# Block-sparse attention into a split-precision MLP on one core: the absolute value of the weight conversion, the fetches of the second matrix and the copies of P are issued at other places

## The chip, the cores and the metric

One core of a Trainium2 chip runs the whole program. The metric is device time in microseconds of one execution: the lower, the better. TensorE (PE) multiplies, with its weight loads shown as PEld; VectorE (DVE), ScalarE (ACT) and GpSimd (POOL) do the rest, and DMAs are issued from the queues of SyncE (SP), POOL and ACT.

## What is computed

Attention over 4 batches, 8 heads, 768 positions of 64 values, with a block mask (blocks of 32: neighbours, first and last block row and column, and three sampled blocks for each row of blocks), and behind it a two-matrix MLP with a sigmoid gate:

```python
scores = np.where(mask, scale * np.matmul(q, k.transpose(0, 1, 3, 2)), -1000000000.0)
attn = np.exp(scores - np.max(scores, axis=-1, keepdims=True))
attn = attn / (np.sum(attn, axis=-1, keepdims=True) + 1e-09)
attn_out = np.matmul(attn, v)
x = attn_out.transpose(0, 2, 1, 3).reshape(B * S, H * D)      # 3072 x 512
h = x @ w_in                                                  # 512 x 2048
g = h * (1.0 / (1.0 + np.exp(-1.702 * h)))
return g @ w_out                                              # 2048 x 512
```

The two weight matrices reach the kernel as 64-bit floating-point words, and the kernel turns them itself into pairs of 32-bit numbers.

## The kernel before

The 3072 tokens are worked on in six chunks of 512. The MLP of a chunk runs over 16 slices of the 2048 inner features; one slice is one turn of `tick(m)`, so ticks 0 to 15 are the first chunk. A tick has four quarters. `up(m)` multiplies the chunk by slice m of `w_in` (12 matmuls), `gate(m)` forms the product g (a tanh on ACT, a copy of the bank to SBUF on ACT in ticks 0 to 12, a multiplication on DVE), and `down(m - 1)` multiplies the slice before by its slice of `w_out`. From slice 8 on g is split: `gate_hi` is a cast on ACT, `gate_lo` a subtraction on DVE at the start of the next tick, and `down` has 12 matmuls of which the last four (line 635) need the low part of g.

Attention of the next chunk is woven in by `plan`, which gives quarters of ticks to its parts. In the first chunk an item's scores stand in quarters 8, 14, 20, 26, 32, 38, 44, 50 and 56, its transposes four quarters behind, and with the scores of an item go the values of the item before (64 small matmuls, line 379). Scores (line 304) and transposes (line 355) use the same two PSUM banks, 0 and 1: the scores can start only when `pt`, ACT's two copies of the transposed P (line 360), has left both. The smallest score is found on DVE (line 327), the four exponentials follow on ACT (line 339). After the last transposes of an item `turn` copies the normalised output into x: a high part on ACT (line 455), a low part on DVE (line 456).

In the same ticks the weights are converted by a generator, `weights()`, `self.conv` in `tick`. It has 32 steps k, in `todo`: step 0 is slice 0 of `w_in`, odd k are slices (k + 1) / 2 of `w_in`, even k are slices k / 2 - 1 of `w_out`, and step 31 is the last slice of `w_out`. A step asks for words to come (`fetch`, a 512 KB DMA on POOL's queue), shifts the absolute value of step k (line 515, DVE), rounds the word of step k - 1 (`rounded`, line 496, ACT), subtracts for its low part (`rest`, line 500, DVE), puts the sign in (line 521, DVE), takes the absolute value of step k + 1 (`first`, line 493, ACT), and puts the low bits in (line 529, DVE). Slices of `w_out` are also written back to DRAM from SP's queue (`ws`, line 535). Slices 0 to 7 of `w_out` need no rounding. `yield` stands between these parts, and `tick` says how many yields are run at each place: `n0` behind the first quarter, `n1` inside `gate`, between the copy of the bank and the multiplication, `n2` at the end. They are 0, 4, 2 in ticks 5, 8, 11 and 14; 2, 4, 4 in ticks 3, 6, 9 and 12; 2, 4, 3 in ticks 4, 7, 10, 13 and 15; 0, 4, 2 in tick 2.

Before the absolute value of a slice f of `w_out` the generator yields as long as the ring of finished slices has no room; `self.downs` is m in tick m once `down(m - 1)` has been issued, and `down` stands between `gate` and the `n2` yields:

```python
while todo[k + 1][1] == 1 and (not self.turned or todo[k + 1][0] - (4 if todo[k + 1][0] < NFULL else WRING) > self.downs - 1):
    yield
```

The tile `a` of the absolute value has two buffers, so from step 18 on that of step k + 1 takes the place of that of step k - 1. The words of `w_out` come into `raw`, which has three buffers; from slice 8 on the converted word stays in it until it has been written back and split. POOL's queue also holds the gathers of the sampled rows of V (line 256), two for each pair of items, issued in `begin` when the values of an item have let go of their buffers.

In ticks 4, 7, 10 and 13 the transposes and the `turn` stand in the third quarter, and there the two copies of P and the copies of `turn` are issued inside `gate`. Everything is issued in the order of the program on each engine.

Of the kernel before, what the change touches and what calls it, by code (L numbers as in the profile page):

```python
# [13 lines left out]
ALU = mybir.AluOpType  # L14
# [24 lines left out]
BIG = float(2 ** 33)  # L39
SCALE = 1.0 / float(D) ** 0.5  # L40
REBASE = 2.0 ** -112
AHEAD = 5
NFULL = 8
FIRST = CU // 2
ORDER = """G0 G1 G2 G3 S0 L0 E0 S1 L1 T0 E1 X1 C0 S2 T1 C1 L2 S3 V0 V1 L3 E2 N0 X2 N1 R0 Y3 E3 T2 R1 X3 C2 H1 T3 H0 S4 Y1 L4 S5 L5
# [4 lines left out]
class Kernel:  # L50
# [411 lines left out]
    def weights(self):  # L462

        nc = self.nc
        todo = []
        for f in range(NF + LAG):
            if f < NF:
                todo.append((f, 0))
            if f >= LAG:
                todo.append((f - LAG, 1))  # L470
        self.ready = set()
        tiles = {}

        def fetch(k):
            if k < len(todo):
                f, i = todo[k]
                if i == 0:
                    raw = self.const.tile([P, 2 * DM], I32, name=f"win{f}")
                else:
                    raw = self.work.tile([P, 2 * DM], I32, name="raw", bufs=3)  # L480
                nc.gpsimd.dma_start(out=raw, in_=self.w64[i][f])
                tiles[k] = {"raw": raw.rearrange("p (a b) -> p a b", b=2)}

        def first(k):


            f, i = todo[k]
            if i == 0 or f >= NFULL:
                a = self.work.tile([P, DM], I32, name="a")
            else:  # L490
                a = self.work.tile([P, DM], F32R, name=("ghi", "glo")[f % 2]).bitcast(I32)
            tiles[k]["a"] = a
            nc.scalar.activation(out=a.bitcast(F32), in_=tiles[k]["raw"][:, :, 1].bitcast(F32), func=AF.Abs, scale=REBASE)

        def rounded(k):
            nc.scalar.copy(out=tiles[k]["to"][:, 0:DM], in_=tiles[k]["w"])

        def rest(k):
            t, w = tiles[k]["to"], tiles[k]["w"]
            nc.vector.tensor_tensor(out=t[:, DM:2 * DM], in0=w, in1=t[:, 0:DM].bitcast(F32), op=ALU.subtract)  # L500
            self.ready.add(todo[k])

        for k in range(3):
            fetch(k)
        yield
        for k in range(3, AHEAD):
            fetch(k)
        yield
        first(0)
        yield  # L510
        for k, (f, i) in enumerate(todo):
            fetch(k + AHEAD)
            raw, a = tiles[k]["raw"], tiles[k]["a"]
            low, high = raw[:, :, 0], raw[:, :, 1]
            nc.vector.tensor_scalar(out=a, in0=a, scalar1=3, scalar2=None, op0=ALU.logical_shift_left)
            if k > 0 and "to" in tiles[k - 1]:
                rounded(k - 1)
                yield
                rest(k - 1)
            yield  # L520
            nc.vector.scalar_tensor_tensor(out=a, in0=high, scalar=-0x80000000, in1=a, op0=ALU.bitwise_and,
                                           op1=ALU.bitwise_or)
            if k + 1 < len(todo):
                while todo[k + 1][1] == 1 and (not self.turned or todo[k + 1][0] - (4 if todo[k + 1][0] < NFULL else WRING) > self.downs - 1):
                    yield
                first(k + 1)
            yield
            w = a if (i, f >= NFULL) != (1, True) else raw.rearrange("p a b -> p (a b)")[:, 0:DM]
            nc.vector.scalar_tensor_tensor(out=w, in0=low, scalar=29, in1=a, op0=ALU.logical_shift_right,
                                           op1=ALU.bitwise_or)  # L530
            w = tiles[k]["w"] = w.bitcast(F32)
            if i == 0:
                self.win[f] = tiles[k]["to"] = self.const.tile([P, 2 * DM], F32R, name=f"win{f}")
            else:
                nc.sync.dma_start(out=self.ws[f], in_=w)
                if f < NFULL:
                    self.whole[f] = w
                    self.ready.add((f, i))
                else:
                    tiles[k]["to"] = self.wout[f % WRING]  # L540
            yield
        rounded(len(todo) - 1)
        rest(len(todo) - 1)
        yield
# [195 lines left out]
    def tick(self, m):  # L740

        n0, n1, n2 = 0, 0, 0
        if m < NF:
            has = lambda part, at: any(part == p for q in at for p, g in self.at.get(q, ()))
            quarter = QT * m
            heavy = has(self.scores, range(quarter, quarter + QT))
            n0, n1, n2 = (0, 4, 4) if heavy else ((2, 2, 5), (2, 4, 1))[m] if m < 2 else (2, 4, 3)
            if has(self.transposes, [quarter]) and heavy:
                n0 = 2
            if has(self.transposes, [quarter + QT]) and has(self.scores, [quarter]):  # L750
                n2 = 2

        def run(n):
            for _ in range(n):
                next(self.conv, None)

        def finish(todo):
            for f in todo:
                f()

        moe = m < NC * NF
        self.gate_lo(m - 1)
        after = self.begin(QT * m)
        finish(after)
        run(n0)
        if moe:
            self.up(m, range(0, 2))
        finish(self.begin(QT * m + 1))
        if moe:
            self.up(m, range(2, 4))  # L770
        after = self.begin(QT * m + 2)
        parts = [[part for part, g in self.at.get(QT * m + q, ())] for q in (2, 3, 4)]
        if m < NF and self.turn in parts[0] and self.values in parts[1] + parts[2]:
            self.gate(m, lambda: (run(n1), finish(after[:2] + after[3:])))
            after = after[:3]
        elif moe:
            self.gate(m, lambda: run(n1))
            finish(after[:2])
        else:
            finish(after[:2])  # L780
        self.down(m - LAG, 0)
        if moe:
            self.gate_hi(m)
        finish(after[2:])
        finish(self.begin(QT * m + 3))
        self.down(m - LAG, 1)
        self.split(m + 1)
        self.stream(m + 3)
        run(n2)
# [141 lines left out]
```

## Time and profile before

| | |
|---|---|
| median of 3 runs | 755.73 us (755.47 to 756.55) |
| the profiled execution, its own time | 755.67 us |
| its span | 754.0 us |
| PE busy | 730.1 us (97%) |
| DVE busy, ACT busy, POOL busy | 405.6 us (54%), 375.7 us (50%), 70.4 us (9%) |
| DMA | 126.87 MB, mean 168 GB/s |

Times in the trace are counted from the start of the span. A row of a timeline gives the start, the length, the engine, the line of the kernel, the operation with its output and inputs, and in brackets how long the engine was idle before it and what ended that. The instructions of one engine overlap at their ends, so two starts may be closer than the length of the first.

### The profile page before, as it was taken

How to read it: one execution, taken by the hardware profiler on the slowest of the kernel's cores; microseconds unless marked ns; L12 is line 12 of the kernel's file. 1: busy time of each engine (PE TensorE's matmuls, PEld its weight loads, DVE VectorE, ACT ScalarE, POOL GpSimd, SP SyncE). 2: the span in 40 equal slices, each digit the busy share in tenths (PEclk: the TensorE clock that was granted, in tenths of full speed). 3: DMA queues.
4: the chain of work that ended last, by engine and by line, in shares of the span. 5: the costliest groups of instructions: out<-in, count | busy, mean ns of one | idle time of the engine just before them, and what ended most of it. 6: DMA issues, size and time to landing. Idle time of an engine off the chain costs nothing.

```text
span 754.0 us, 18913 instructions
## 1 busy us (share of the span) xinstructions
PE 730.1 (97%) x7424; PEld 562.6 (75%) x7424; DVE 405.6 (54%) x1069; ACT 375.7 (50%) x939; POOL 70.4 (9%) x111
## 2 busy tenths in 40 slices
PE   3989999999999999999999999999999999999997
PEld 1665667777787777788778778778777777888885
DVE  3778879885554445454454454354555344443332
ACT  2766667765464454444445445444554454333232
POOL 4333212120000000000000000000000000000000
PEclk9999999999999999999999999999999999999999
DMA  8999996685642547554444564445564321041111
GB/s 240 304 372 363 334 329 200 228 254 176 237 162 82 170 155 212 154 178 149 122 150 147 150 172 155 127 141 155 185 222 141 106 77 43 30 112 43 56 43 56
DMA packets 64250, 126.87 MB, mean 168 GB/s; under 512 B 7617, under 2 KB 30402, under 8 KB 63650
## 3 DMA queue, kind: packets, MB, share of 16 engines
q1 hardware_dynamic: 51922, 83.72, 36.0%
q0 software_dynamic: 11376, 41.03, 16.1%
q8 instruction: 58, 0.95, 0.5%
q10 hardware_dynamic: 864, 0.93, 0.4%
q14 instruction: 30, 0.25, 0.1%
HBM read 115.16 MB, written 10.49 MB: 167 GB/s over the span
## 4 chain that ended last, share of the span: by engine, by line
PE 92%; DVE 3%; ACT 2%; issue 1%; DMA 1%; SPq 0%; ACTq 0%
PE bank L579 12%; PE bank L580 11%; PE bank L581 11%; PE bank L639 11%; PE bank L635 11%; PE bank L640 11%; PE bank L304 6%; PE bank L355 6%; PE bank L379 5%; PE bank L624 3%; PE bank L399 2%; PE bank L316 2%; PE bank L448 2%; DMA scratch<-in_sampled_blocks_dram 1%; DMA vmid<-in_v_dram 1%
## 5 line engine op out<-in xcount | busy, mean ns | idle before, releaser
L594 DVE SCALAR_TENSOR_TENSOR g<-g,bank 128x512 f32<-128x512 f32 x83 | 57.1, 688 | 169.3 <-ACT g L587 169.2
L339 ACT ACTIVATE ex<-bank,nm 128x256 f32<-128x256 f32 (+1 forms) x176 | 84.8, 491 | 119.8 <-DVE nm L327 119.8
L639 PE MATMUL bank<-wout,ghi 128*128 128x512 f32 x352 | 139.2, 396 | 0.0
L640 PE MATMUL bank<-wout,ghi 128*128 128x512 f32 x352 | 136.7, 388 | 0.0
L587 ACT ACTIVATE g<-bank 128x512 f32<-128x512 f32 x96 | 57.6, 600 | 147.0 <-PE bank L581 147.0
L562 DVE TENSOR_TENSOR wout<-wst,wout 128x512 fp32r<-128x512 f32 x80 | 55.4, 692 | 78.9 <-ACT wout L561 77.9
L635 PE MATMUL bank<-wout,glo 128*128 128x512 f32 x352 | 97.0, 388 | 0.0
L327 DVE CUSTOM_DVE_ANT_1 bank<-bank,bias 128x256 f32<-128x256 f32 x176 | 73.7, 440 | 21.4 <-PE bank L304 9.7
L579 PE MATMUL bank<-xhi,win 128*128 128x512 f32 x192 | 79.7, 415 | 0.5 <-ACT xhi L455 0.5
L601 ACT CAST ghi<-g 128x512 fp32r<-128x512 f32 x88 | 54.8, 623 | 47.7 <-DVE g L594 47.7
L579 PE MATMUL bank<-x,win 128*128 128x512 f32 x192 | 77.7, 405 | 0.0
L635 PEld LDWEIGHTS bank<-wout,glo 128*128 128x128 f32 x352 | 66.1, 188 | 13.9
L639 PEld LDWEIGHTS bank<-wout,ghi 128*128 128x128 f32 x352 | 66.1, 188 | 13.0
L640 PEld LDWEIGHTS bank<-wout,ghi 128*128 128x128 f32 x352 | 66.2, 188 | 12.8
L580 PE MATMUL bank<-xlo,win 128*128 128x512 f32 x192 | 74.9, 390 | 0.0
L581 PE MATMUL bank<-xhi,win 128*128 128x512 f32 x192 | 74.8, 390 | 0.0
L581 PE MATMUL bank<-x,win 128*128 128x512 f32 x192 | 74.7, 389 | 0.0
L580 PE MATMUL bank<-x,win 128*128 128x512 f32 x192 | 74.7, 389 | 0.0
L256 POOL DMA_INDIRECT vown<-in_v_dram,vidx x40 | 39.9, 997 | 371.9 <-PE bank L379 258.5
L360 ACT COPY pt<-bank 128x512 f32<-128x512 f32 (+1 forms) x112 | 57.0, 565 | 20.3 <-PE bank L355 20.2
L304 PE MATMUL bank<-kg,qt 64*32 64x256 f32 x1280 | 48.4, 399 | 13.3 <-DMA vmid<-in_v_dram 11.9
L609 DVE TENSOR_TENSOR glo<-g,ghi 128x512 fp32r<-128x512 f32 x88 | 60.3, 685 | 1.4 <-ACT ghi L601 1.4
(140 smaller groups left out, 1047.8 us busy)
## 6 DMA issues: line engine op xcount, KB each, us to landing
wst<-ws SPq DMA_DIRECT2D x80, 256.0 KB
kg<-in_kb_dram SPq DMA_DIRECT2D x114, 128.0 KB
kg<-in_kb_dram SPq DMA_DIRECT2D x42, 256.0 KB
win<-in_moe_w_in_dram POOLq DMA_DIRECT2D x16, 512.0 KB
raw<-in_moe_w_out_dram POOLq DMA_DIRECT2D x16, 512.0 KB, 7.0
kg<-in_kT_dram SPq DMA_DIRECT2D x4, 1536.0 KB
vown<-in_vd_dram SPq DMA_DIRECT2D x8, 768.0 KB
out_dram<-raw SPq DMA_DIRECT2D x41, 128.0 KB
```

What stands on the lines that cost most here:

```text
L304: nc.tensor.matmul(sps[h][BLK * c:BLK * (c + 1), n * i:n * (i + 1)].rearrange("p (g n s) -> p g n s", g=2, s=BLK), self.qt[r][rows, bi, UT ...
L327: nc.vector.tensor_tensor_reduce(out=at, in0=at, in1=bias, scale=-SCALE, scalar=3.0e38, op0=ALU.add, op1=ALU.min, accum_out=un["nm"][:, ha ...
L339: nc.scalar.activation(out=ex, in_=sps[h][:, n * k:n * (k + 1)], func=AF.Exp, bias=un["nm"][:, half, c:c + 1], scale=-1.0, accum_out=un["r ...
L579: nc.tensor.matmul(to, wih[:, k], xh, start=(k == 0), stop=False)
L580: nc.tensor.matmul(to, wih[:, k], xl, start=False, stop=False)
L581: nc.tensor.matmul(to, wil[:, k], xh, start=False, stop=(k == NCT - 1))
L587: nc.scalar.activation(out=g, in_=self.h, func=AF.Tanh, scale=0.851)
L594: nc.vector.scalar_tensor_tensor(out=g, in0=g, scalar=1.0, in1=h, op0=ALU.add, op1=ALU.mult)
L609: self.nc.vector.tensor_tensor(out=glo, in0=g, in1=ghi.bitcast(F32), op=ALU.subtract)
L635: nc.tensor.matmul(to[n], glo[:, tk[n]], woh, start=False, stop=last)
L639: nc.tensor.matmul(to[n], ghi[:, tk[n]], woh, start=(f == 0), stop=False)
L640: nc.tensor.matmul(to[n], ghi[:, tk[n]], wol, start=False, stop=False)
```

## The change

Three edits. In the generator the absolute value of step k + 1, with the loop that waits for room ahead of it, is issued behind the low part of step k - 1 and ahead of the yield, no longer behind the sign of step k. The words of slices 8 to 15 of `w_out` are asked for three steps ahead in place of five (everything else still five). In the third-quarter case of `tick` the two copies of P are issued ahead of the conversion's `n1` yields and no longer behind them; the copies of `turn` stay behind.

```diff
-AHEAD = 5
+AHEAD, NEAR = 5, 3
...
         def fetch(k):
-            if k < len(todo):
+            if k < len(todo) and k not in tiles:
...
-            fetch(k + AHEAD)
+            fetch(k + NEAR)
+            if k + AHEAD < len(todo) and (todo[k + AHEAD][1] == 0 or todo[k + AHEAD][0] < NFULL):
+                fetch(k + AHEAD)
...
                 rounded(k - 1)
                 yield
                 rest(k - 1)
-            yield
-            nc.vector.scalar_tensor_tensor(out=a, in0=high, scalar=-0x80000000, in1=a, op0=ALU.bitwise_and,
-                                           op1=ALU.bitwise_or)
             if k + 1 < len(todo):
                 while todo[k + 1][1] == 1 and (not self.turned or todo[k + 1][0] - (4 if todo[k + 1][0] < NFULL else WRING) > self.downs - 1):
                     yield
                 first(k + 1)
+            yield
+            nc.vector.scalar_tensor_tensor(out=a, in0=high, scalar=-0x80000000, in1=a, op0=ALU.bitwise_and,
+                                           op1=ALU.bitwise_or)
             yield
...
-            self.gate(m, lambda: (run(n1), finish(after[:2] + after[3:])))
+            self.gate(m, lambda: (finish(after[:2]), run(n1), finish(after[3:])))
             after = after[:3]
```

## Rows read from the trace of the kernel before

**Rows 1.** PE's waits: line, releaser, us in total, times, longest.

```profile
PE bank L379 <- issue: 2.4, 7, 0.4
```

**Rows 2.** Timeline of PE: start, length, instruction, idle before.

```profile
74.64 1.58 PE L304 MATMUL bank<-kg,qt 64*32 64x256 f32 x32 [0.75 <-ACT pt L360]
...
125.77 1.09 PE L304 MATMUL bank<-kg,qt 64*32 64x256 f32 x32
...
127.82 0.49 PE L639 MATMUL bank<-wout,ghi 128*128 128x512 f32 x1
...
136.32 1.07 PE L635 MATMUL bank<-wout,glo 128*128 128x512 f32 x4
137.32 1.53 PE L304 MATMUL bank<-kg,qt 64*32 64x256 f32 x32
...
149.53 1.09 PE L304 MATMUL bank<-kg,qt 64*32 64x256 f32 x32
...
153.71 0.50 PE L639 MATMUL bank<-wout,ghi 128*128 128x512 f32 x1
```

**Rows 3.** Timeline of POOL from 149 to 151 us.

```profile
149.59 0.53 POOL L481 DMA_DIRECT2D raw<-in_moe_w_out_dram  x1 [8.31 <-DMA ws<-raw]
150.43 1.09 POOL L256 DMA_INDIRECT vown<-in_v_dram,vidx  x1 [0.30 <-issue]
```

**Rows 4.** Timeline of DVE, steps 7, 18 and 19 of the conversion.

```profile
71.02 0.44 DVE L515 TENSOR_SCALAR a<-a 128x512 int32<-128x512 int32 x1 [1.41 <-ACT a L493]
...
112.43 0.69 DVE L500 TENSOR_TENSOR wout<-raw,wout 128x512 fp32r<-128x512 f32 x1 [0.57 <-ACT wout L496]
...
117.93 0.68 DVE L500 TENSOR_TENSOR win<-a,win 128x512 fp32r<-128x512 f32 x1
```

**Rows 5.** Timeline of ACT, ticks 3, 7, 8, 9 and 10.

```profile
73.48 0.62 ACT L496 CAST win<-a 128x512 fp32r<-128x512 f32 x1 [1.91 <-DVE a L529]
...
111.75 0.65 ACT L496 CAST wout<-raw 128x512 fp32r<-128x512 f32 x1
...
113.49 0.75 ACT L493 ACTIVATE a<-raw 128x512 f32<-128x512 f32 x1
...
116.92 0.48 ACT L339 ACTIVATE ex<-bank,nm 128x256 f32<-128x256 f32 x1 [0.64 <-DVE nm L327]
...
122.61 1.05 ACT L360 COPY pt<-bank 128x512 f32<-128x512 f32 x2
...
136.52 1.09 ACT L360 COPY pt<-bank 128x512 f32<-128x512 f32 x2
```

**Rows 6.** Timeline of ACT, tick 11.

```profile
142.26 0.48 ACT L339 ACTIVATE ex<-bank,nm 128x256 f32<-128x256 f32 x1 [1.56 <-DVE nm L327]
...
144.08 0.60 ACT L587 ACTIVATE g<-bank 128x512 f32<-128x512 f32 x1
144.56 0.60 ACT L592 COPY wst<-bank 128x512 f32<-128x512 f32 x1
145.03 0.70 ACT L493 ACTIVATE a<-win 128x512 f32<-128x512 f32 x1
...
146.82 0.63 ACT L601 CAST ghi<-g 128x512 fp32r<-128x512 f32 x1 [0.59 <-DVE g L594]
```

**Rows 7.** Timeline of DVE, tick 11.

```profile
141.16 0.42 DVE L327 CUSTOM_DVE_ANT_1 bank<-bank,bias 128x256 f32<-128x256 f32 x1
...
143.27 0.68 DVE L500 TENSOR_TENSOR win<-a,win 128x512 fp32r<-128x512 f32 x1
143.87 0.69 DVE L521 SCALAR_TENSOR_TENSOR a<-raw,a 128x512 int32<-128x512 int32 x1
144.59 0.69 DVE L529 SCALAR_TENSOR_TENSOR raw<-raw,a 128x512 int32<-128x512 int32 x1
...
146.10 0.69 DVE L594 SCALAR_TENSOR_TENSOR g<-g,wst 128x512 f32<-128x512 f32 x1
```

**Rows 8.** DMA issues of the page: size, median us to landing.

```profile
raw<-in_moe_w_out_dram POOLq DMA_DIRECT2D x16, 512.0 KB, 7.0
```

## The prediction

> **What bounds the kernel now.** I read the table of engines first: PE is busy for 730.1 of 754.0 us, so only its idle time, or time in which it waits with a matmul counted as running, can be won. The busy time by stretches and PE's waits came next. Most idle time lies before 53 us, which the change hardly touches. Then PE's timeline of the first chunk's ticks, where it loses time at these places, all in [rows 2]. At 74.64 the scores of quarter 14 wait 0.75 us for P's copies and take 1.58 us in place of 1.09: 1.24 lost. At 137.32 (quarter 44) they take 0.44 us too long. Quarters 20 and 32 lose some 0.2 together. In tick 12 the way from scores to the first matmul of `down` is 4.18 us (149.53 to 153.71) where tick 9 has 2.05 (125.77 to 127.82): 2.13 lost among the 64 small matmuls of the values, as "issue", a wait for nothing the profile shows [rows 1]. Then the timelines of ACT, DVE and POOL around these places.
>
> How much room P's copies need: in tick 10 they start at 136.52 [rows 5], 0.80 us ahead of the scores, and 0.44 is lost. So **the copies must start 1.24 us ahead of the scores**, and each missing bit is PE's loss.
>
> **The absolute value, early.** In tick 2 DVE idles 1.41 us for the absolute value of step 7 [rows 4], which stands on ACT behind the exponentials and the gate. That delays the low bits of step 7, and ACT idles 1.91 us for those ahead of rounding 7 at 73.48 [rows 5], with P's copies of quarter 12 queued behind it. With the change the absolute value is issued in tick 1, ahead of the exponentials, where ACT has idle time. The chain gets some 1.4 us shorter, P's copies start before 72.6, and the scores of quarter 14 no longer wait: -1.24. No instruction is added or lost, and DVE's order stays; ACT's changes only where a run of yields ends between the old and the new place.
>
> **A yield lost, late.** The waiting loop moves as well. In tick 7 the absolute value of step 20 (slice 9) finds no room: 9 - 3 > 6 - 1. Before, the four yields inside `gate` were the low bits of 18, rounding 18, its low part, then the sign of 19 and the loop's yield; row 113.49 is that absolute value, issued only behind `down` [rows 5]. Now the third and fourth both go to the loop, and the sign of 19 comes behind `down`. From here on the conversion is one yield behind. That moves rounding 19 from the end of tick 7 into `gate` of tick 8, on ACT behind the four exponentials, the tanh and the copy; before, its low part ran on DVE beside them (117.93, [rows 4]). DVE, which must do it before the sign of 20, now idles. The same happens after the exponentials of quarters 38, 44, 50 and 56.
>
> **What that costs.** Start to start, from tick 11 [rows 6, 7] and tick 7: four exponentials 1.82 (142.26 to 144.08); an ACT copy, cast or tanh 0.5; a pair of P's copies 0.95; ACT to the DVE instruction that waits for it 0.68 (111.75 to 112.43); DVE to the next 0.60, or 0.72 where that reads the result; DVE to ACT 0.72 (146.10 to 146.82); first minimum to first exponential 1.10. I count on the clock of the trace before; ACT and DVE of tick 6 wait for PE, so what PE gains before it shifts all alike.
>
> Tick 7: P's copies go ahead of rounding 18 (third edit), so its low part is 0.95 later; one short DVE shift (step 20) drops out behind. The exponentials of quarter 32 start some 0.6 later, 117.5 for 116.92 [rows 5].
>
> Tick 8: exponentials 1.82, tanh and copy 0.95, rounding 19 to its low part 0.68, sign 0.60, low bits 0.72, product 0.60, cast of g 0.72, rounding 20 0.5, absolute value 22 0.5, next 0.57: 7.66. P's copies of quarter 36 start at 125.15 in place of 122.61. The scores are due at 125.77: 0.62 of room where 1.24 is needed. Loss 0.6.
>
> Tick 9: 7.5 us more of the same chain (copies 0.95, `turn` 0.8, sign and low bits 1.44, rounding 21 and its low part 1.4, sign and low bits 1.3, product 0.6, minimum and exponentials from it 1.1) put the exponentials of quarter 38 at 132.6; they end at 134.5. Then cast of g, rounding 22, its low part, sign and low bits 23 (3.0), and only then the low part of g 9, done at 138.2. The matmuls that need it were due at 136.32 + 0.6 [rows 2]: loss 1.3.
>
> Tick 10: rounding 23, its low part, absolute value 25 (which waits for that low part, its buffer), tanh, copy: P's copies of quarter 42 at 140.6. The scores were due at 137.32 + 0.6 + 1.3 = 139.2. They need copies at 138.0: loss 2.6. The 0.44 of before is in it.
>
> Tick 11: 6.5 us from there to the exponentials (147.1), the 7.66 of tick 8 to P's copies of quarter 48 (154.8). Scores due at 149.53 + 0.6 + 1.3 + 2.6 - 0.4 = 153.6: loss 2.4.
>
> Ticks 12 to 15, by the same sums and with less certainty: 1.3 for the low part of g 12, 0.7 at quarter 56 (no copy of the bank there any more), 2.1 at the scores of tick 15, behind which the conversion is done. Sum of losses 0.6 + 1.3 + 2.6 + 2.4 + 4.1 = 11.0.
>
> **Fetches.** On POOL the gathers of tick 11 stand behind the last `raw` fetch, which waits 8.31 us until slice 12 has been written back: 149.59, and the gather follows at 150.43 [rows 3], exactly beside the values of tick 12. With three steps ahead the last two fetches stand behind these gathers, which go out right after the values of tick 11, beside large matmuls. I take the 2.13 us as due to that coincidence, since no other gather after 53 us runs beside the values of an item, and none of these stalls: -2.13; if it is not so, 0. Fetch to landing is 7.0 us [rows 8], and the words, asked for later but less held up in the queue, arrive before their absolute value is due: 0. The writes on SP shift with the low bits; POOL alone waits for them.
>
> The Trainium skill speaks against this edit: its page "SBUF — State Buffer", section "SBUF: two separate sides", says that engine ports and DMA ports are disjoint, so that a transfer cannot slow a matmul. The trace shows four gaps among these matmuls at that very time, which the rule does not explain. By the rule the stall has another cause and may stay, and the sum is 2.13 higher.
>
> **The third edit** has no cost but the 0.95 in tick 7 (there in the sum) and wins the 0.2 of quarters 20 and 32; the 0.44 of quarter 44 is overtaken by the lost yield.
>
> Sum: -1.24 - 0.2 - 0.44 - 2.13 = -4.0, +11.0: **+7.0 us**, on the profiled execution's 755.67 (the median is 755.73) **762.7 us**.
>
> **Rivals.**
>
> *The room suffices: faster.* It is decided in tick 8: if P's copies of quarter 36 still start 1.24 us ahead (by 124.5), because rounding 19 is ready sooner or DVE makes up the idle time, the chain stays behind PE's pace and no loss follows. For it: DVE is busy for 54% of the span, and the copies had 3.16 us of room (122.61 against 125.77). Against: the chain of tick 8 grows from 5.69 to 7.66 us by durations that repeat all over the trace. 755.7 - 4.0 = 751.7.
>
> *The gather is not the cause*, the stall in tick 12 stays: 764.8. For it: the idle time is "issue", and the mechanism is not visible. Against: the coincidence.
>
> *Losses end early, no change:* if PE's own lateness gives ACT and DVE room again after quarter 44, the losses are 4.5, which the 4.0 cancel: 756.2. Against: in tick 11 ACT and DVE wait for each other, not for PE, so they gain nothing when PE is late.
>
> **How the numbers follow.** A difference under 0.2% (1.5 us) can't be told from none here. Forecast with the stall gone 0.55, with the stall kept 0.11: both slower, 0.66. Losses ending early 0.12. Room suffices 0.22. So faster 0.22, same 0.12, slower 0.66. The forecast's own range is 759 to 766: each loss ahead of tick 12 is known to some 0.3, those behind it may be half or a quarter more. The whole range reaches from 752.0, which leaves out half of the faster case, to 767.0, above which some 0.07 lie.
>
> **What would show it.** Right: at quarter 14 the scores take 1.09 without idle time; rounding 19 stands behind the exponentials of quarter 32, and DVE idles some 2 us ahead of its low part; PE waits for P's copies in ticks 9, 11 and 12, and for the low part of g in 10 and 13; the values of tick 12 take 1 us, with the gathers ahead of them, right behind the values of tick 11. Wrong: rounding 19 ahead of these exponentials, or P's copies of quarter 36 over 1.24 us ahead of the scores: then it is faster, and the late ticks look as before.

## The result, and the profile after

The changed kernel takes 766.4 us (763.52 to 768.35, 6 runs) against 755.6 us (754.01 to 757.98, 6 runs): ratio 1.0142, 95% interval 1.0115 to 1.017. It is slower. It lies 3.7 us above the forecast of 762.7 us and just above the 759 to 766 that the prediction gave for this case, inside its whole range, which reaches to 767.0. The profiled execution took 765.96 us, with a span of 764.3. From line 480 on the changed kernel's lines are two higher than those of before: the low part of g is L611, the low bits L531, the product L596.

First, PE's waits between 54 and 200 us: line, releaser, us in total, times, longest.

```profile
PE bank L637 <- DVE glo L611: 1.9, 2, 1.0
PE bank L304 <- ACT pt L360: 1.9, 1, 1.9
PE bank L581 <- DVE g L596: 1.2, 1, 1.2
...
PE bank L355 <- ACT ex L339: 0.3, 2, 0.2
```

The line of [rows 1] counts the whole span; of its seven waits as "issue" the kernel before had three in this stretch:

```profile
PE bank L379 <- issue: 1.1, 3, 0.4
```

These are gone, and waits for DVE and ACT have come. PE's timeline after shows where:

```profile
76.19 1.09 PE L304 MATMUL bank<-kg,qt 64*32 64x256 f32 x32
...
126.96 1.57 PE L304 MATMUL bank<-kg,qt 64*32 64x256 f32 x32
...
139.50 1.21 PE L637 MATMUL bank<-wout,glo 128*128 128x512 f32 x4 [0.92 <-DVE glo L611]
142.59 2.54 PE L304 MATMUL bank<-kg,qt 64*32 64x256 f32 x32 [1.87 <-ACT pt L360]
...
152.25 1.07 PE L637 MATMUL bank<-wout,glo 128*128 128x512 f32 x4
...
157.16 1.58 PE L304 MATMUL bank<-kg,qt 64*32 64x256 f32 x32
158.66 0.32 PE L379 MATMUL bank<-vmid,pt 128*32 128x64 f32 x8
...
159.47 0.29 PE L379 MATMUL bank<-vown,pt 128*32 128x64 f32 x8
...
161.62 1.07 PE L637 MATMUL bank<-wout,glo 128*128 128x512 f32 x4
...
169.69 1.21 PE L637 MATMUL bank<-wout,glo 128*128 128x512 f32 x4 [0.99 <-DVE glo L611]
170.83 1.61 PE L304 MATMUL bank<-kg,qt 64*32 64x256 f32 x32
...
181.38 0.50 PE L581 MATMUL bank<-xhi,win 128*128 128x512 f32 x1 [1.16 <-DVE g L596]
```

Row 76.19 is quarter 14: no idle time, 1.09 us [rows 2]. Quarter 38 (126.96) takes 1.57, the low part of tick 10 is waited for 0.92, quarter 44 waits 1.87 and takes 2.54. Behind them the low part is waited for again in tick 13, and in tick 15 `up` waits for the product of the tick before, which reads the PSUM bank that `up` is to fill. The values of tick 12 run from 158.66 to 159.76 without a gap. Before, they took three times as long, with PE idle three times:

```profile
151.64 0.22 PE L379 MATMUL bank<-vmid,pt 128*32 128x64 f32 x1 [0.40 <-issue]
...
152.41 0.29 PE L379 MATMUL bank<-vown,pt 128*32 128x64 f32 x3 [0.42 <-issue]
...
153.26 0.24 PE L379 MATMUL bank<-vown,pt 128*32 128x64 f32 x1 [0.32 <-issue]
```

ACT after, and below it DVE, in ticks 8 to 12:

```profile
118.62 0.47 ACT L339 ACTIVATE ex<-bank,nm 128x256 f32<-128x256 f32 x1 [3.40 <-DVE nm L327]
...
121.38 0.65 ACT L496 CAST win<-a 128x512 fp32r<-128x512 f32 x1
...
126.35 1.04 ACT L360 COPY pt<-bank 128x512 f32<-128x512 f32 x2
...
141.93 1.09 ACT L360 COPY pt<-bank 128x512 f32<-128x512 f32 x2
...
156.54 1.05 ACT L360 COPY pt<-bank 128x512 f32<-128x512 f32 x2
```

```profile
122.06 0.69 DVE L500 TENSOR_TENSOR win<-a,win 128x512 fp32r<-128x512 f32 x1 [2.02 <-ACT win L496]
...
138.76 0.69 DVE L611 TENSOR_TENSOR glo<-g,ghi 128x512 fp32r<-128x512 f32 x1
```

Rounding 19 (121.38) stands behind the exponentials of quarter 32, and DVE idles 2.02 us for it. From the exponentials to P's copies of quarter 36 it takes 7.73 us; the copies start 0.61 us ahead of the scores.

Not all of the distance lies there. Tick 0 begins later in this execution than in that of before, where its first matmul starts at 53.52 us:

```profile
55.89 0.49 PE L581 MATMUL bank<-xhi,win 128*128 128x512 f32 x1 [0.46 <-ACT xhi L455]
```

I therefore count each kernel from there: span less the start of this matmul, called its *run* below. It is 754.0 - 53.52 = 700.5 us before and 764.3 - 55.89 = 708.4 after: **+7.9**.

### The profile page after: what moved, and what is told of

Read it like the earlier page. It is cut to its first block, busy times and chain, and to the rows that moved or that the text cites. A ratio compares the mean times of both kernels' runs of the same rounds, so it can differ in the third digit from the quotient of the medians.

```text
span 764.3 us, 18912 instructions
## 1 busy us (share of the span) xinstructions
PE 733.2 (96%) x7424; PEld 563.0 (74%) x7424; DVE 406.3 (53%) x1069; ACT 374.4 (49%) x939; POOL 68.8 (9%) x111
## 4 chain that ended last, share of the span: by engine, by line
PE 85%; DVE 6%; ACT 5%; issue 2%; another core or an unknown queue 1%; DMA 1%; ACTq 0%; DVEq 0%
PE bank L581 11%; PE bank L582 11%; PE bank L583 11%; PE bank L641 10%; PE bank L637 10%; PE bank L642 10%; PE bank L355 5%; PE bank L379 5%; PE bank L304 5%; PE bank L626 2%; PE bank L399 2%; PE bank L316 2%; PE bank L448 2%; DVE a L527 1%; ACT ex L339 1%
## 5 line engine op out<-in xcount | busy, mean ns | idle before, releaser
L596 DVE SCALAR_TENSOR_TENSOR g<-g,bank 128x512 f32<-128x512 f32 x83 | 57.1, 688 | 169.6 <-ACT g L589 169.5
L641 PEld LDWEIGHTS bank<-wout,ghi 128*128 128x128 f32 x352 | 66.1, 188 | 12.9
L611 DVE TENSOR_TENSOR glo<-g,ghi 128x512 fp32r<-128x512 f32 x88 | 60.2, 684 | 0.7 <-ACT ghi L603 0.7
```

The costliest lines, as they stand in the source:

```text
L596: nc.vector.scalar_tensor_tensor(out=g, in0=g, scalar=1.0, in1=h, op0=ALU.add, op1=ALU.mult)
L611: self.nc.vector.tensor_tensor(out=glo, in0=g, in1=ghi.bitcast(F32), op=ALU.subtract)
L641: nc.tensor.matmul(to[n], ghi[:, tk[n]], woh, start=(f == 0), stop=False)
```

## Experiments

### The three edits one by one

Edit 1 alone (absolute value and waiting loop ahead of the sign):

> The first edit alone: absolute value and waiting loop issued ahead of the sign; fetches five ahead and P's copies behind the conversion, as before. Theory (the moved waiting loop takes a yield of the conversion in tick 7, and from there on it runs behind): the whole loss is here. Rounding 19 stands behind the exponentials of quarter 32, PE waits for P's copies at the scores of quarters 44 and 50 and for the low part of g in ticks 10 and 13: 764 to 768 us against 755.6, +1.1 to +1.6%. Rival (the loss comes from the later fetches or from P's copies pushing the conversion back): no such waits, 754 to 756 us, since only the gain of 1.24 us at quarter 14 is left.

Measured: 764.06 us, ratio 1.0112 (1.0092 to 1.0133); run 708.1, +7.6. The waits are those of the changed kernel: 0.96 us for the low part in tick 10, 2.41 for P's copies at quarter 44. The loss is edit 1's. The values of tick 12 don't stall here either, though the fetches are still five ahead: with the conversion one yield late the last fetch falls behind the gathers anyway.

Edit 2 alone:

> The second edit alone: words of slices 8 to 15 of w_out three steps ahead. Theory (the small matmuls of the values stall when a gather of V runs beside them): the gathers of tick 11 go out behind the values of tick 11, the 64 matmuls of the values of tick 12 take 1 us in place of 3.1: 753.5 us, -0.2 to -0.3%. Rival (a transfer can't slow PE; the stall has another cause): the values of tick 12 still take about 3 us and the time is 755.6. Second rival (words arrive too late): PE waits for a conversion late in the first chunk, slower than 755.6.

754.65 us, ratio 0.9981 (0.9964 to 0.9999); run 698.7, -1.8. The gathers go out at 141.94 and 143.23, and the values of tick 12 take 1.0 us.

Edit 3 alone:

> The third edit alone: P's copies ahead of the conversion in the third quarter of ticks 4, 7, 10 and 13. Theory: quarters 20, 32 and 44 win 0.2 + 0.44 us, and the 0.95 us by which rounding 18 comes later in tick 7 is hidden: 755.0 us, -0.1%, with the scores of quarter 44 at 1.1 us in place of 1.53. Rival (the 0.95 us carries on through the tight chain of ticks 8 to 12): P's copies of quarter 36 start near 123.5 in place of 122.6, still ahead of what is needed, but the low part of g or P's copies of quarter 48 come late, 756 to 758 us.

757.28 us, ratio 1.0017 (1.0004 to 1.0031); run 701.0, +0.5. Neither theory: no scores behind quarter 14 wait for P's copies, quarters 20 and 44 win 0.2 and 0.3 us, and what is late is the low part that `turn` makes. PE's waits from 54 to 200 us, and DVE in tick 7:

```profile
PE bank L379 <- DVE x L456: 1.5, 2, 1.0
```

```profile
114.45 0.69 DVE L500 TENSOR_TENSOR wout<-raw,wout 128x512 fp32r<-128x512 f32 x1 [1.53 <-ACT wout L496]
115.06 0.68 DVE L521 SCALAR_TENSOR_TENSOR a<-win,a 128x512 int32<-128x512 int32 x1
115.66 0.42 DVE L456 TENSOR_TENSOR x<-bank,x 128x256 fp32r<-128x256 f32 x1
```

With rounding 18 behind P's copies DVE idles 1.53 us for it in place of 0.57 [rows 4], and the low part of x (L456) stands behind it. It reads the bank into which the values of tick 8 are to be written: they wait 0.5 us, those of tick 11 1.0. (That the run is only 0.5 longer has a second reason: the values of tick 12 stalled 0.7 us less here than in the profile of before.)

### The yields

All edits kept, but where there is no room the absolute value goes the old way (`waits` is the condition of the loop):

```diff
-            if k + 1 < len(todo):
-                while todo[k + 1][1] == 1 and (...):
-                    yield
-                first(k + 1)
+            room = k + 1 < len(todo) and not waits(k + 1)
+            if room:
+                first(k + 1)
             yield
             nc.vector.scalar_tensor_tensor(out=a, in0=high, scalar=-0x80000000, in1=a, op0=ALU.bitwise_and,
                                            op1=ALU.bitwise_or)
+            if k + 1 < len(todo) and not room:
+                while waits(k + 1):
+                    yield
+                first(k + 1)
```

> The changed kernel, but where the absolute value finds no room it is issued in the old way, sign first and the waiting loop behind it, so no yield is lost; all three edits are kept otherwise. Theory (the lost yields are the whole loss): ACT's order in ticks 8 to 15 is that of before, no waits of PE in ticks 9 to 15, and the gains remain: 751.7 to 752.5 us, -0.4 to -0.5%. Rival (the later fetches, the copies or the early absolute value itself slow the late ticks): 757 us or more.

755.62 us, ratio 1.0006 (0.9991 to 1.0021), no gain in the time where 751.7 to 752.5 was expected; run 699.25, -1.2. The waits of ticks 9 to 15 for P's copies and for the low part of g are gone, so the loss is the yields'. The run gains 1.2 in place of 3 to 4; the 1.5 us of edit 3 are there again (0.5 and 1.0 for `x`), and 0.4 for a product.

The other way round: before, with one yield fewer.

```diff
+            if m == 7:
+                n2 = 2
```

> The kernel before with none of the three edits; only the yields at the end of tick 7 are 2 in place of 3. Theory (one lost yield in tick 7 is by itself enough for the loss): the conversion runs one yield behind from tick 8 on, PE waits for P's copies at the scores of quarters 44 and 50 and for the low part of g in ticks 10 and 13, and the time counted from the first matmul of tick 0 grows by some 9 to 11 us: 764 to 767 us. Rival (the loss needs the other parts of the change, or the conversion catches up one yield within a tick or two): 756 to 758 us.

760.11 us, ratio 1.0043 (1.0023 to 1.0063); run 703.4, +2.9. PE's timeline, ticks 10 and 11:

```profile
139.11 1.21 PE L635 MATMUL bank<-wout,glo 128*128 128x512 f32 x4 [0.85 <-DVE glo L609]
142.52 1.68 PE L304 MATMUL bank<-kg,qt 64*32 64x256 f32 x32 [2.19 <-ACT pt L360]
```

These are the changed kernel's waits of the same place. But behind quarter 44 no loss follows: the scores of quarters 50 and 56 take 1.09. (The stall in tick 12 is there, 0.7 us shorter than in the profile of before, so these waits cost some 3.6.) So one lost yield is not the whole loss, and the theory had to be mended. Counted through the program, the loop takes one yield in tick 7 and one in tick 10 before. Here it takes none in tick 10: the late conversion finds room at once, and is on time again. In the changed kernel the loop stands one yield earlier. It takes two in tick 7, and one in tick 10 though the conversion is late. The slack that would let it catch up is used to wait.

The changed kernel with a yield given back, in tick 7 (first) or in tick 10 (second):

```diff
+            if m == 7:      # 10 in the second
+                n2 = 4
```

> The changed kernel with one yield given back at the end of tick 7 (4 in place of 3); nothing else. ACT's order is then that of the kernel without lost yields up to tick 10, where the waiting loop takes the next yield. Theory (each turn of the waiting loop costs a yield, and what follows costs what it cost behind tick 7): no waits of PE before tick 12; behind it P's copies of quarters 50 and 56 and the low part of g late as before, 4 to 5 us lost in place of 11: 757 to 760 us. Rival (the loss was set in tick 7 alone): 752 to 754 us. Second rival (the loss has nothing to do with the yields): 766 us.

761.11 us, ratio 1.0068 (1.0047 to 1.0088); run 704.2, +3.8. Little is lost up to quarter 44: 0.4 us each for P's copies there and for the values behind it, which wait for the low part of x. In tick 10 the loop takes two yields, and behind it PE waits 1.5 us for P's copies at quarter 50, 1.0 for the low part in tick 13, 0.9 for the product in tick 15. The median is 1.1 above what was expected.

> The changed kernel with one yield given back at the end of tick 10 (4 in place of 3), not of tick 7. Theory (the change stays slow because its waiting loop takes a yield again in tick 10, where the kernel with one lost yield alone caught up): PE waits in ticks 10 and 11 as in the changed kernel (low part of g 0.9 us, P's copies at quarter 44 some 2 us), none at quarter 50 and in tick 13's low part of g: 2 to 4 us above before from the first matmul of tick 0, 758 to 760 us. Rival (after tick 7 the lateness keeps itself going, a yield more or less does not help): 765 us or more.

760.74 us, ratio 1.007 (1.0046 to 1.0094); run 703.8, +3.3. PE waits 0.96 and 1.89 us in ticks 10 and 11, and at quarters 50 and 56 and in tick 13 not at all. So this kernel has the loss of ticks 8 to 11 and not what follows; the mended theory holds, though the median is 0.7 above what it gave.

### The stall of the values

> The kernel with the second edit alone, but the two gathers of tick 11 are held on POOL until the low part of g of tick 11 is there (a copy of four columns of it stands ahead of them), so that they run beside the scores and values of tick 12. Theory (a gather beside the small matmuls stalls them): the gathers start at about 151 and 152.2 us, and the values of tick 12, 1.0 us long without the hold, take 2 to 3 us, as issue. Rival (the stall belongs to the words' fetch that stood ahead of the gathers, or to something else): the values take 1.0 us, whatever the gathers do.

```diff
+        if self.held:
+            self.nc.gpsimd.tensor_copy(out=self.seen[:, 0:4], in_=self.g[m - 1][2][:, 0:4].bitcast(F32))
+            self.gather(self.held.pop())
```

(Cut from this diff: in `begin` the gathers of tick 11 are put into `held` and not issued.) One execution, 754.87 us; run 699.8, 1.1 more than with edit 2 alone. POOL and then PE:

```profile
149.30 0.99 POOL L260 DMA_INDIRECT vown<-in_v_dram,vidx  x1 [0.56 <-PE bank L587]
150.60 0.96 POOL L260 DMA_INDIRECT vown<-in_v_dram,vidx  x1 [0.30 <-issue]
151.56 0.59 POOL L485 DMA_DIRECT2D raw<-in_moe_w_out_dram  x1
```

```profile
150.14 0.32 PE L383 MATMUL bank<-vmid,pt 128*32 128x64 f32 x8
...
151.36 0.32 PE L383 MATMUL bank<-vmid,pt 128*32 128x64 f32 x5 [0.41 <-issue]
152.14 0.23 PE L383 MATMUL bank<-vmid,pt 128*32 128x64 f32 x1 [0.45 <-issue]
...
152.90 0.50 PE L645 MATMUL bank<-wout,ghi 128*128 128x512 f32 x1
```

The gaps are back, the values take 2.8 us in place of 1.0, and the first gap lies ahead of the fetch of words (151.56). The converse:

```diff
-            fetch(k + AHEAD)
+            if k + AHEAD < len(todo) - 1:
+                fetch(k + AHEAD)
+            if k + 4 == len(todo) - 1:
+                fetch(k + 4)
```

> The kernel before, but the last fetch of words is issued four steps ahead in place of five, so that it stands on POOL behind the gathers of tick 11 and no longer ahead of them; it still waits for slice 12 to be written back. Theory (the gathers stall the values): the gathers go out near 142 us, the last fetch still near 150, and the values of tick 12 take 1.0 us; 2 us less than before from the first matmul of tick 0. Rival (the fetch of 512 KB itself, or its wait, stalls the values): 3 us for the values, as before.

One execution, 753.28 us; run 698.8, -1.7. The gathers go out at 139.75 and 141.05, the last fetch at 151.17, just behind the values, which take 1.0 us. That a fetch beside them does no harm is seen in the changed kernel: its last one is issued 0.33 us after the scores of quarter 50 start, and the values show no gap. POOL there:

```profile
147.28 0.98 POOL L256 DMA_INDIRECT vown<-in_v_dram,vidx  x1 [6.76 <-PE bank L379]
148.57 0.97 POOL L256 DMA_INDIRECT vown<-in_v_dram,vidx  x1 [0.31 <-issue]
149.54 0.58 POOL L481 DMA_DIRECT2D raw<-in_moe_w_out_dram  x1
157.49 0.56 POOL L481 DMA_DIRECT2D raw<-in_moe_w_out_dram  x1 [7.37 <-DVE rg L420]
```

### The start, and the clock

> The changed kernel once more, unchanged, for a second profile. Two readings of the first one are at stake. If the 2.4 us by which its tick 0 began later belong to that execution, tick 0 starts between 53.4 and 55.3 us now, as in the other profiles; if they belong to the change, near 55.9 again. If the fall of TensorE's granted clock to 0.5 behind the waits of ticks 10 and 11 follows from these waits, it is there again, and the scores of quarter 44 take 2.5 us; if it was chance, they take 1.6.

One execution, 764.45 us; tick 0 begins at 54.40, the run is again 708.4. So the late start belonged to that execution. The clock falls again, and quarter 44 takes 2.16.

```diff
+            if k == 0:
+                first(1)
...
-                first(k + 1)
+                if k > 0:
+                    first(k + 1)
```

> The kernel before with one instruction moved: the absolute value of step 1 is issued ahead of the sign of step 0, so on ACT it stands ahead of P's four copies at the start, as in the changed kernel; everything behind is as before. Theory (part of the 10.8 us between the medians is the start: from the first matmul of tick 0 on the changed kernel loses 7.9, and the kernels with this early place were on average 1.2 us further above before, in their medians, than that count says): 756.3 to 757.5 us, +0.1 to +0.2%. Rival (the start differs by chance alone, with the time at which the first words land): 755.6 us, same as before.

756.01 us, ratio 1.0004 (0.9989 to 1.002): no cost can be told. Tick 0 began between 52.8 and 55.9 us over all these profiles, with no order by kernel. But the medians lie 10.8 us apart (8.7 to 12.9 by the interval) where the runs differ by 7.9, and in all ten kernels with four executions or more the median stands 0.6 to 2.9 us further above before than the run does. Part of this is the one profile of before, against which every run is counted: the kernel with step 1 moved, the same from tick 0 on, has a run of 699.7, 0.75 less, with 0.7 less of the stall in tick 12. Small differences of runs are no better known than that; the other 2 us of the changed kernel stay open.

### A version that beats both

Edit 2, edit 1 with the old way where there is no room and in step 0 (`room = 0 < k < len(todo) - 1 and not waits(k + 1)` in the diff above), edit 3 undone:

> Meant to beat both kernels: the fetches three ahead (second edit); the absolute value issued early only where there is room for it, and not in step 0 (so the start has ACT's old order); P's copies behind the conversion again (third edit undone). Theory (the third edit makes the low part of x late, for which the values of ticks 8 and 11 waited 0.5 and 1.0 us; without it the gains of 1.2 us at quarter 14 and 1.8 in tick 12 stay whole): 752.5 to 753.0 us, -0.3 to -0.4% and 3 us less from the first matmul of tick 0 to the end. Rival (the gains are given back elsewhere): 754.5 to 756 us.

754.43 us against 756.22, ratio 0.997 (0.9948 to 0.9992); run 697.6, -2.9. The run is as expected, the median 1.4 above. Between 54 us and the end one wait of PE is left:

```profile
PE bank L588 <- ACT xhi L455: 0.5, 1, 0.5
```

## Why the prediction held, step by step

What PE lost or won from tick 0 on, by how far the rows after stand behind those of before, less the 2.37 us of the start:

| step of the prediction | predicted | measured |
|---|---|---|
| quarters 14, 20, 32 | -1.44 | -1.43 |
| scores of quarter 38 | +0.6 | +0.7 |
| low part of g 9 | +1.3 | +1.5 |
| P's copies of quarter 42, with the 0.44 | +2.2 | +2.1 |
| clock in tick 11 | not foreseen | +2.3 |
| P's copies of quarter 48 | +2.4 | +0.5 |
| values of tick 12 | -2.13 | -2.13 |
| low part of g 12 | +1.3 | +1.5 |
| quarter 56 | +0.7 | +0.7 |
| tick 15, and to the end | +2.1 | +2.2 |
| sum | +7.0 | +7.9 |

So of the 3.7 us between forecast and median these steps account for 0.9. The rest lies outside them: in the profile of before and in what is open above.

**The lost yield.** Right to the place: rounding 19 behind the exponentials, 7.73 us to P's copies where 7.66 were counted, room of 0.61 where 0.62 was. The rival that room suffices falls with it. "From here on the conversion is one yield behind" needed a reason that the prediction did not give: the run with a yield lost alone catches up in tick 10, and only the place of the loop keeps the changed kernel late. The outcome was right and that step incomplete.

**Quarter 48 against the clock.** Two terms are wrong and nearly cancel: 2.4 us were predicted at quarter 48, where 0.5 came, and none for the clock, which the prediction took as in the trace of before and which cost 2.3. The windows of the profile after; columns: stretch, its length, busy us of PE, PEld, DVE, ACT and POOL, granted clock, DMA share, GB/s:

```profile
140.00:142.00 2.00, 0.71 (x4) 0.22 (x2) 1.97 (x4) 1.58 (x4) 0.53 (x1) 0.89 0.42 94
142.00:144.00 2.00, 1.41 (x19) 0.95 (x26) 0.48 (x2) 1.81 (x5) 0.00 (x0) 0.50 0.75 295
144.00:146.00 2.00, 2.00 (x59) 1.19 (x47) 1.97 (x6) 0.77 (x2) 0.00 (x0) 0.50 0.02 8
146.00:148.00 2.00, 2.00 (x43) 1.64 (x33) 1.93 (x6) 0.45 (x1) 0.72 (x1) 0.50 0.03 8
148.00:150.00 2.00, 2.00 (x10) 1.62 (x9) 1.80 (x8) 1.59 (x7) 1.69 (x3) 0.91 0.74 201
```

Near the end of the second of the two waits, 0.92 and 1.87 us, the clock falls to 0.50, the lower of its two levels (1.2 GHz), until 148: the scores take 2.54, the values 1.9 us in place of 1.0, the first matmuls of `up` start 0.4 to 0.6 apart in place of 0.2 to 0.3. PE comes 2.3 us later to quarter 50, so P's copies (156.54) are 0.62 ahead of it and only 0.5 is lost there. The runs of the changed kernel with much and with less of this fall (quarter 44 at 2.54 and 2.16) are equal, 708.4: what PE lost to the clock it did not wait for ACT; in the second profile, where the clock took less, it waits 0.43 us for P's copies at quarter 50. So the sum fits, but not by the route that was predicted.

**The values.** The size was right against this profile of before, whose stall is the longest of five. That the gather is the cause is shown: with the second edit kept, moving the gathers back beside the values (behind a small copy on POOL) brought the gaps back, and a fetch beside them alone did not. The rival that the gather is not the cause falls. Credit to the second edit was wrong: the first alone moves the gathers, so inside this change no gain is left that the second could claim. The Trainium skill's rule ("SBUF — State Buffer", section "SBUF: two separate sides") that a transfer cannot slow a matmul would let the gathers run beside the values at no cost; here they cost PE 1.4 to 2.1 us, and the measurement decides. Whether they meet in SBUF or elsewhere stays open: the gaps are "issue", a wait for nothing that the profile shows.

**The third edit.** "No cost but the 0.95 in tick 7" failed: alone it costs 1.5 us at the values of ticks 8 and 11, through the low part of x on DVE, which the prediction had not followed. In the changed kernel this wait doesn't show. In tick 8 the lost yield has taken the sign of 19 out from ahead of the low part of x; in tick 11 the scores run at the lower clock and end later. Where they took 1.68 us there (the yield back in tick 10), the values wait 0.39 for x.

**Losses end early** falls too: the losses of tick 13 and tick 15 came in full. In tick 15 it is not the scores that wait first but `up`, for a product that reads the bank.

## What to carry to other kernels

A waiting loop that yields is part of a schedule: move it, and count for each tick how many yields it takes and what work these would have done, also in the later ticks where its waiting is the slack that a late chain needs. When an instruction goes ahead of others in an in-order queue, follow what stands behind it on the engine that waits for those others, up to the bank or buffer that PE wants next. Count a profile from a fixed instruction behind the start; here it took 3 us of scatter out of a comparison over 8. And profile the kernel before twice: every difference is counted against it.

## What the runs showed of the hardware

Two waits of PE, of 0.9 to 1.0 and 1.9 to 2.4 us, close together, went with a fall of the clock to 0.50 in four profiles (the changed kernel's two, edit 1 alone, and the yield back in tick 10), by the windows for 3.4 to 6.8 us. One window each of the second profile of the changed kernel, of edit 1 alone and of the yield back in tick 10 (columns as above):

```profile
144.00:146.00 2.00, 2.00 (x58) 1.76 (x51) 1.93 (x6) 1.21 (x2) 0.22 (x1) 0.52 0.09 29
142.00:144.00 2.00, 2.00 (x47) 1.01 (x34) 1.93 (x6) 1.06 (x2) 0.00 (x0) 0.50 0.57 223
144.00:146.00 2.00, 2.00 (x46) 1.71 (x39) 1.97 (x5) 1.57 (x3) 0.59 (x1) 0.50 0.10 31
```

In the kernel with one yield lost, waits of 0.85 and 2.19 us at the same place left it at 1.00:

```profile
140.00:142.00 2.00, 0.32 (x2) 0.00 (x0) 1.63 (x3) 1.34 (x4) 1.04 (x2) 1.00 0.31 45
142.00:144.00 2.00, 1.48 (x32) 0.84 (x32) 1.44 (x3) 1.23 (x3) 0.00 (x0) 1.00 0.83 258
```

What decides between the two is open. And an indirect gather issued from POOL beside 64 small matmuls cost these 1.4 to 2.1 us in each of the five profiles where the two met (quarter 50 to quarter 56 took 12.96 to 13.68 us), and nothing where they did not (11.55 or 11.56 in five others).
